# Attention scores moved out of PSUM by halves, a third bank for the other matmuls, and a wait on GpSimd

## The chip, the cores and the metric

The kernel runs on one core of a Trainium2 chip. The metric is the device time of one execution in microseconds (us), the median of several runs. A profiled execution, taken apart from these, gives the trace that the text reads. Engines are named as in the profile: PE is TensorE (matmuls), PEld its loading of weights, DVE VectorE, ACT ScalarE, POOL GpSimd, SP SyncE, which issues the DMAs.

## The reference

Two layers that have nothing to do with each other, written side by side. All data is fp32.

```python
def _A_ref(x, wqkv, wo):                       # x 1 x 2048 x 1024
    H = 32; Dh = D // H                        # 32 heads of 32
    q, k, v = ...(x @ wqkv)...                 # three projections
    scores = einsum("bhqd,bhkd->bhqk", q, k) * Dh ** -0.5
    p = softmax(scores, axis=-1)               # 2048 x 2048 for each head
    o = einsum("bhqk,bhkd->bhqd", p, v)
    return o.transpose(...).reshape(B, S, D) @ wo

def _B_ref(x, dft_seq_re, dft_seq_im, dft_hid_re, dft_hid_im):
    a = einsum("bsd,ed->bse", x, dft_hid_re)
    b = einsum("bsd,ed->bse", x, dft_hid_im)
    return einsum("ts,bse->bte", dft_seq_re, a) - einsum("ts,bse->bte", dft_seq_im, b)

return concatenate([_A_ref(...), _B_ref(...)], axis=-1)
```

## The kernel before

**Three kinds of work on TensorE.** Dense products (the projections of q, k and v, both products of the Fourier layer, the output projection) are done by a scheme of seven products for every block of 2 x 2. Each factor is split into a high and a low part of TensorE's fast fp32 format (`halves`: a cast `high`, line 477, and a subtraction `low`, line 480), and three matmuls stand for one. Sums of blocks that a product needs are made at line 455. These matmuls (line 391) are called *fills*; a group of 12 or 24 of them adds up in one PSUM bank of 128 x 512, and one VectorE instruction moves it out (lines 629 to 681, 894 to 907).

Attention goes by heads and has three streams. *S* (line 1198): a tile of scores, 128 queries by 1024 keys, in the PSUM tile `psS`. VectorE (line 1206) moves it to an SBUF row `srow`, negated, and takes the row minimum on the way into `negm`; ScalarE (line 1212) takes the exponentials, of which only the sums are used. So S gives each query's maximum and the sum of its exponentials. For head 0 VectorE only reduces (line 1208) and ScalarE works in PSUM (line 1214). *T* (line 1328): the transposed scores, keys by queries, with the maximum already taken off by two more rows of the product, in the banks `psT`; ScalarE makes the exponentials `pt`, `ptl` (line 1332). *V* (line 1347): products of these with V, 4096 short matmuls in all, 40, 40 and 48 in a block for each head; VectorE gathers the block into `ot` (lines 1358 and 1360).

S of head h + 1 runs while T and V of head h do, with fills between them. Before the first head there are only fills, and behind the last head the output projection.

**The order is planned while the program is written.** The class `Plan` simulates the engines with a duration for each operation (`MM`, `PV`, `SWITCH` and so on, in us) and emits each instruction when its engine is free in the plan and its inputs are ready. The chip then runs each engine's queue in that order, and semaphores hold an instruction until its inputs are there. The plan picks the next matmul from the heads of the streams S, T, V and the next fill, so that fills keep step with attention (the main loop, from line 1408). `LATE` and `SLATE` are how long the plan waits after the planned release of an input before it issues a matmul (`SLATE` for S). `OVERLAP` is what the next instruction of an engine may start early. A subtraction or a sum may go to GpSimd (`SUB`) or VectorE (`ADD`), whichever the plan finds free.

**The port.** Operations marked `two` use an SBUF port that VectorE and GpSimd share in the plan: `Plan.port` is the time at which it becomes free, and `choose` starts no GpSimd operation, nor a VectorE operation marked `two`, before that. On the chip nothing holds them apart in the kernel before: a GpSimd instruction starts when its own inputs are there.

**PSUM.** There are eight banks. Before: two tiles `psS` of two banks each, two banks `psT`, two banks `psD`. The tile `pd` of `psD` takes fills and V; `bank()` picks where a fill's group goes, and as long as attention isn't under way fills take `psT` too. The main loop keeps count of the banks in use (`banks`, at most 2, or 4 without attention).

Of the kernel before, what the change touches and what calls it, by code (L numbers as in the profile page):

```python
# [62 lines left out]
class Plan:  # L63
# [6 lines left out]
    OVERLAP = {"ACT": 0.13, "DVE": 0.08, "POOL": 0.08}  # L70
# [4 lines left out]
    QUEUE = 1.0  # L75

    def __init__(self):
        self.now = 0.0
        self.free = {e: 0.0 for e in ("PE", "ACT", "DVE", "POOL", "SP")}
        self.pending = {e: [] for e in ("ACT", "DVE", "POOL", "SP")}  # L80
        self.able = {e: [] for e in ("ACT", "DVE", "POOL", "SP")}
        self.dma = 0.0
        self.port = 0.0
        self.lane = [0.0] * 8
        self.seq = 0

# [39 lines left out]
    def start(self, o, e=None):  # L126
        e = e or o.engine
        o.emit(e) if o.other else o.emit()
# [83 lines left out]
def kernel(  # L212
# [79 lines left out]
    def load_qk(h, which, j):  # L292
# [12 lines left out]
        for n, b in (("psD", 2), ("psT", 2), ("psS", 2))  # L305
# [32 lines left out]
    MM, PV, SWITCH, TINY = 0.2275, 0.853, 0.40, 0.17  # L338
    ES, ET = 1.235, 0.625
    MOVE = 1.25  # L340
# [4 lines left out]
    LATE, SLATE = 0.25, 1.2  # L345
    HB = 0
    ACAST = 0.6
    RES = 400
    SST = 13
# [9 lines left out]
    pl = Plan()  # L359
    op = pl.op  # L360
# [56 lines left out]
    def fetch(shape, terms, store=None, keep=None):  # L417
# [23 lines left out]
        for sign, *term in terms[1:]:  # L441
# [12 lines left out]
            def add(e, sign=sign, other=other, a=None if last is not None else first[0]):  # L454
                (nc.gpsimd if e == "POOL" else nc.vector).tensor_tensor(  # L455
# [13 lines left out]
    def halves(raw, made, users, hi, lo, old, mine, order=(None, None)):  # L469
# [3 lines left out]
        def high(e=None):  # L473
            if e == "ACT":
                nc.scalar.activation(hi(), raw(), AF.Copy)
            else:
                nc.vector.tensor_copy(hi(), raw())  # L477

        def low(e):
            (nc.gpsimd if e == "POOL" else nc.vector).tensor_tensor(out=lo(), in0=raw(), in1=f(hi()), op=ALU.subtract)  # L480
# [679 lines left out]
    psS_r, psT_r, pt_r, vt_r, rt_r, ot_r = Ring(2), Ring(2), Ring(NPT), Ring(2), Ring(1), Ring(2)  # L1160
    small = {n: Ring(b) for n, b in (("st", 2), ("nm", 2), ("lh", 2), ("tw", 1))}
    qx_r = Ring(1)
    row_r = Ring(NROW)
    got = {}
# [7 lines left out]
    def scores(h):  # L1172
# [12 lines left out]
        for n, (qt, c) in enumerate([(k % 4, k // 4) for k in range(8)] + [divmod(k, 2) for k in range(8, 32)]):  # L1185
            old, users = psS_r.take()
            own = h > 0 and qt < 4
            box = {}
            if h:
                rold, ruse = row_r.take()  # L1190

            def mm(n=n, qt=qt, c=c, box=box, own=own):
                if n == 0:
                    ST["negm"] = sm.tile([P, 2, NS], F32, name="negm", bufs=2)
                    ST["sums"] = sm.tile([P, 2, NS], F32, name="sums", bufs=2)
                box["p"] = p = psS.tile([P, 1024], F32, name="psS")
                for i in range(2):
                    nc.tensor.matmul(  # L1198
                        p[:, i * NB : i * NB + NB], (QX[0] if own else QS[h % 2])[:, qt * P : qt * P + P],
                        KS[h % 2][:, c * 1024 + i * NB : c * 1024 + i * NB + NB], start=True, stop=True,  # L1200
                    )

            def mx(qt=qt, c=c, box=box):
                if h:
                    box["s"] = att_low().tile([P, 1024], F32, name="srow", bufs=NROW)
                    nc.vector.tensor_scalar(box["s"], box["p"], -1.0, None, op0=ALU.mult, op1=ALU.min, accum_out=ST["negm"][:, c, qt : qt + 1])  # L1206
                    return
                nc.vector.tensor_reduce(out=ST["negm"][:, c, qt : qt + 1], in_=box["p"], axis=AX.X, op=ALU.max, negate=True)  # L1208

            def ex(qt=qt, c=c, box=box):  # L1210
                if h:
                    nc.scalar.activation(box["s"], box["s"], AF.Exp, scale=-1.0, bias=ST["negm"][:, c, qt : qt + 1], accum_out=ST["sums"][:, c, qt : qt + 1])  # L1212
                    return
                nc.scalar.activation(box["p"], box["p"], AF.Exp, bias=ST["negm"][:, c, qt : qt + 1], accum_out=ST["sums"][:, c, qt : qt + 1])

            a = op("PE", 2 * MM, mm, [*old, *([got.get((h, "x"))] if own else [got.get((h, 0, qt // 4)), got.get((h, "z"))]), got.get((h, 1, 2 * c)), got.get((h, 1, 2 * c + 1))],
                   [users, xuse] if own else [users])
            b = op("DVE", MOVE if h else MAX, mx, [a] + (sold if n == 0 else []) + (rold if h else []), [users, suse, *([ruse] if h else [])], 0)
            e = op("ACT", ES, ex, [b], [ruse if h else users, suse], 0)
            exp_of[a] = e  # L1220
            maxes.append(b)
            exps.append(e)
            Sops.setdefault(h, []).append(a)
            streams["S"].append((a, h, n))
# [11 lines left out]
        def high():  # L1236
            box["l"] = sm.tile([P, 2, NS], F32R, name="lh", bufs=2)
            nc.vector.tensor_reduce(out=box["l"][:, 0], in_=ST["negm"].rearrange("p c n -> p n c"), axis=AX.X, op=ALU.min)

        def low():  # L1240
            nc.vector.tensor_tensor(out=box["l"][:, 1], in0=ST["nm"], in1=f(box["l"])[:, 0], op=ALU.subtract)
# [4 lines left out]
        def across():  # L1246
            box["t"] = sm.tile([P, 2 * NS], F32, name="lt", bufs=2)
# [11 lines left out]
    def sums(h):  # L1259
# [4 lines left out]
        def sub():  # L1264
            box["t"] = sm.tile([P, 2, NS], F32, name="tt", bufs=1)
            for c in range(2):
                nc.vector.tensor_tensor(out=box["t"][:, c], in0=ST["nm"], in1=ST["negm"][:, c], op=ALU.subtract)
# [250 lines left out]
```

## Time and profile before

| | us |
|---|---|
| median of 3 runs | 2990.05 (2988.33 to 2990.17) |
| profiled execution | 2990.43 |
| its span, first to last instruction | 2988.7 |
| PE busy | 2957.1 (99%) |
| DVE busy | 2395.0 (80%) |
| ACT busy | 2301.3 (77%) |
| POOL busy | 930.1 (31%) |
| mean granted TensorE clock | 0.998 of full speed |

The difference between the profiled execution and its span lies around the program. Matmuls are pipelined and the spans of two overlap, so a busy PE is not PE at its peak: what a matmul costs is read from the distance between the starts of two. A wait is shown with the engine whose work came last before it ended. Rows of groups read: line, engine, operation, output<-input, shapes, count | busy us, mean ns of one | idle us before them and who ended it. Rows of the timeline read: start us, duration us, engine, line, operation, count, and in brackets the idle time before it.

### The profile page before, as it was taken

How to read it: one execution, taken by the hardware profiler on the slowest of the kernel's cores; microseconds unless marked ns; L12 is line 12 of the kernel's file. 1: busy time of each engine (PE TensorE's matmuls, PEld its weight loads, DVE VectorE, ACT ScalarE, POOL GpSimd, SP SyncE). 2: the span in 40 equal slices, each digit the busy share in tenths (PEclk: the TensorE clock that was granted, in tenths of full speed). 3: DMA queues.
4: the chain of work that ended last, by engine and by line, in shares of the span. 5: the costliest groups of instructions: out<-in, count | busy, mean ns of one | idle time of the engine just before them, and what ended most of it. 6: DMA issues, size and time to landing. Idle time of an engine off the chain costs nothing.

```text
span 2988.7 us, 45652 instructions
## 1 busy us (share of the span) xinstructions
PE 2957.1 (99%) x14912; PEld 2145.3 (72%) x14912; DVE 2395.0 (80%) x4180; ACT 2301.3 (77%) x4316; POOL 930.1 (31%) x688
## 2 busy tenths in 40 slices
PE   9999999999999999999999999999999999999999
PEld 7887776677677677767776676777777767677787
DVE  7779788688877877887678888888787888887796
ACT  4336887888788888888888888888988888786321
POOL 2315345122212332222112353323212245343142
PEclk9999999999999999999999999999999999999999
DMA  9976657666626644554435675545433586466762
GB/s 338 360 233 201 200 180 249 193 219 218 209 68 200 203 148 142 180 179 145 139 110 155 197 240 170 165 152 171 129 112 99 185 267 211 149 187 200 266 207 99
DMA packets 376582, 558.59 MB, mean 187 GB/s; under 512 B 111100, under 2 KB 111100, under 8 KB 376220
## 3 DMA queue, kind: packets, MB, share of 16 engines
q1 hardware_dynamic: 376344, 555.68, 58.1%
q8 instruction: 117, 1.92, 0.3%
q14 instruction: 121, 0.99, 0.1%
HBM read 402.42 MB, written 153.11 MB: 186 GB/s over the span
## 4 chain that ended last, share of the span: by engine, by line
PE 90%; DVE 3%; ACT 3%; DMA 1%; issue 1%; SPq 0%; POOL 0%; DVEq 0%; POOLq 0%
PE pd L391 40%; PE pd L1347 15%; PE psT L1328 15%; PE psS L1198 14%; PE psT L391 7%; ACT srow L1212 2%; ACT pt L1332 1%; DVE srow L1206 1%; DVE slot L477 1%; DMA c<-u_d 0%; ACT ptl L1332 0%; DMA raw<-in_wd 0%; DVE negm L1208 0%; DVE h L477 0%; DMA rt<-r_d 0%
## 5 line engine op out<-in xcount | busy, mean ns | idle before, releaser
L1206 DVE TENSOR_SCALAR_CACHE_REDUCE srow<-psS 128x1024 f32<-128x1024 f32 x992 | 1203.1, 1220 | 211.2 <-ACT srow L1212 135.8
L1212 ACT ACTIVATE srow<-srow,negm 128x1024 f32<-128x1024 f32 x992 | 1197.1, 1214 | 15.1 <-DVE srow L1206 14.8
L1332 ACT ACTIVATE pt<-psT 128x512 f32<-128x512 f32 x1618 | 924.3, 643 | 254.9 <-PE psT L1328 238.1
L391 PE MATMUL pd<-slot,h 128*128 128x512 f32 x3352 | 1111.4, 391 | 4.8 <-DVE ot L1358 1.8
L1328 PE MATMUL psT<-qs,ks 128*128 128x512 f32 x2048 | 752.5, 396 | 5.6 <-ACT pt L1332 3.5
L391 PEld LDWEIGHTS pd<-slot,h 128*128 128x128 f32 x3352 | 630.1, 188 | 144.7 <-issue 4.2
L391 PE MATMUL pd<-slot,l 128*128 128x512 f32 x1676 | 654.4, 390 | 1.0 <-POOL l L480 1.0
L1328 PEld LDWEIGHTS psT<-qs,ks 128*128 128x128 f32 x2048 | 381.5, 188 | 157.5 <-ACT srow L1212 28.5
L480 POOL TENSOR_TENSOR l<-raw,h 128x512 fp32r<-128x512 f32 x167 | 226.1, 1355 | 796.0 <-DVE h L477 576.9
L1198 PE MATMUL psS<-ks,qs 128*128 128x512 f32 x1552 | 471.1, 391 | 1.3 <-DVE srow L1206 1.2
L1347 PE MATMUL pd<-pt,vt 128*32 128x512 f32 x3236 | 396.6, 597 | 1.6 <-DVE slot L896 1.1
L455 POOL TENSOR_TENSOR raw<-raw,g 128x512 f32<-128x512 f32 x221 | 295.7, 1344 | 317.8 <-issue 58.3
L391 PEld LDWEIGHTS pd<-slot,l 128*128 128x128 f32 x1676 | 315.2, 188 | 68.2 <-POOL l L480 1.8
L1198 PEld LDWEIGHTS psS<-ks,qs 128*128 128x128 f32 x1552 | 290.9, 188 | 63.9 <-DVE srow L1206 3.2
L1332 ACT ACTIVATE ptl<-psT 128x512 f32<-128x512 f32 x430 | 249.0, 639 | 109.7 <-PE psT L1328 102.8
L480 POOL TENSOR_TENSOR slot<-raw,slot 128x512 fp32r<-128x512 f32 x151 | 213.6, 1422 | 355.8 <-DVE slot L477 225.6
L1212 ACT ACTIVATION_READ_ACCUMULATOR srow<-srow,negm 128x1 f32 x992 | 257.7, 260 | 0.0
L1347 PEld LDWEIGHTS pd<-pt,vt 128*32 128x32 f32 x3236 | 102.3, 110 | 191.3 <-issue 182.4
L391 PE MATMUL pd<-slot,slot 128*128 128x512 f32 x768 | 189.6, 391 | 0.2 <-DVE e L681 0.2
L1360 DVE TENSOR_TENSOR ot<-ot,pd 128x512 f32<-128x512 f32 x64 | 43.9, 685 | 161.3 <-PE pd L1347 161.3
L1347 PE MATMUL pd<-ptl,vt 128*32 128x512 f32 x860 | 165.9, 600 | 4.2 <-DVE e L681 3.5
L391 PEld LDWEIGHTS pd<-slot,slot 128*128 128x128 f32 x768 | 144.2, 188 | 31.5 <-DVE e L681 0.5
(126 smaller groups left out, 2451.7 us busy)
## 6 DMA issues: line engine op xcount, KB each, us to landing
raw<-in_ct SPq DMA_DIRECT2D x224, 256.0 KB
g<-in_ct SPq DMA_DIRECT2D x128, 256.0 KB
qk_d<-e SPq DMA_DIRECT2D x52, 512.0 KB
qs<-qk_d SPq DMA_DIRECT2D x128, 192.0 KB
ks<-qk_d SPq DMA_DIRECT2D x128, 192.0 KB
raw<-ab_d SPq DMA_DIRECT2D x96, 256.0 KB
c<-u_d SPq DMA_DIRECT2D x88, 256.0 KB
g<-ab_d SPq DMA_DIRECT2D x80, 256.0 KB
```

The source lines that it names most:

```text
L391: nc.tensor.matmul(box["ps"], a[1]((a[0].hi, a[0].lo)[u]()), b[1]((b[0].hi, b[0].lo)[v]()), start=k == 0, stop=k == n - 1)
L455: (nc.gpsimd if e == "POOL" else nc.vector).tensor_tensor(out=dest(), in0=dest() if a is None else a.get(), in1=other["q"] if "q" in other ...
L477: nc.vector.tensor_copy(hi(), raw())
L480: (nc.gpsimd if e == "POOL" else nc.vector).tensor_tensor(out=lo(), in0=raw(), in1=f(hi()), op=ALU.subtract)
L1198: nc.tensor.matmul(p[:, i * NB : i * NB + NB], (QX[0] if own else QS[h % 2])[:, qt * P : qt * P + P], KS[h % 2][:, c * 1024 + i * NB : c * ...
L1206: nc.vector.tensor_scalar(box["s"], box["p"], -1.0, None, op0=ALU.mult, op1=ALU.min, accum_out=ST["negm"][:, c, qt : qt + 1])
L1212: nc.scalar.activation(box["s"], box["s"], AF.Exp, scale=-1.0, bias=ST["negm"][:, c, qt : qt + 1], accum_out=ST["sums"][:, c, qt : qt + 1])
L1328: nc.tensor.matmul(box["p"], KS[h % 2][:, t * P : t * P + P], QS[h % 2][:, j * NB : j * NB + NB], start=True, stop=True)
L1332: nc.scalar.activation(box["t"], box["p"], AF.Exp)
L1347: nc.tensor.matmul(po["p"][j * DH : j * DH + DH, :], VT[h][:, k, :], box["t"], start=(k == t0), stop=(k == t), tile_position=(0, j * DH),)
L1360: nc.vector.tensor_tensor(out=po["o"], in0=po["o"], in1=po["p"], op=ALU.add)
```

## The change

- A tile of scores is made in two halves of 512 keys, each in a PSUM bank of its own, of which there are three (`psS` 3 x 1 bank in place of 2 x 2). VectorE moves each half. The second half starts its minimum from what the first half left in `negm`, so it reads that value. The exponentials are still taken over the whole row of 1024 for heads 1 to 31. For head 0 VectorE writes the negated scores back to PSUM, and ScalarE takes the exponentials by halves; their sums are added up later.
- `psD`, for fills and V, has three banks in place of two; the main loop's counts follow (3 and 5).
- When the plan starts a GpSimd operation, and the last port-using VectorE operation that it started ends in the plan later than 2.5 us ago (`NEAR`), the GpSimd instruction gets a wait for that VectorE instruction (`behind`). For that, functions that emit now return their instruction.
- Planned durations: `PV` 0.853 to 0.86, `SWITCH` 0.40 to 0.30, `ES` 1.235 to 1.31 and `OVERLAP` of ACT 0.13 to 0.15, `ET` 0.625 to 0.64, `MOVE` 1.25 for a tile to 0.70 for a half, `ACAST` 0.6 to 0.63. `SLATE` 1.2 to 0.25, `SST` 13 to 14.
- The small tiles `lh` and `lt` have one buffer in place of two.

```diff
-    OVERLAP = {"ACT": 0.13, "DVE": 0.08, "POOL": 0.08}
+    OVERLAP = {"ACT": 0.15, "DVE": 0.08, "POOL": 0.08}
+    NEAR = 2.5
...
+        if e == "DVE" and o.two:
+            self.held = made, self.free[e]
+        elif e == "POOL" and self.held is not None and self.held[1] > self.now - self.NEAR:
+            self.behind(made, self.held[0])
...
-        for n, b in (("psD", 2), ("psT", 2), ("psS", 2))
+        for n, b in (("psD", 3), ("psT", 2), ("psS", 3))
...
-    MM, PV, SWITCH, TINY = 0.2275, 0.853, 0.40, 0.17
-    ES, ET = 1.235, 0.625
-    MOVE = 1.25
+    MM, PV, SWITCH, TINY = 0.2272, 0.86, 0.30, 0.17
+    ES, ET = 1.31, 0.64
+    MOVE = 0.70
...
-    LATE, SLATE = 0.25, 1.2
+    LATE, SLATE = 0.25, 0.25
-    ACAST = 0.6
+    ACAST = 0.63
-    SST = 13
+    SST = 14
...
+    pl.behind = lambda a, b: tc.add_manual_dep(a.ins, b.ins.name, ...)
...
-        if (not att_on[0] or not t_on[0]) and nbank[0] % 4 < 2:
+        if (not att_on[0] or not t_on[0]) and nbank[0] % 5 < 2:
...
-    psS_r, ... = Ring(2), ...
+    psS_r, ... = Ring(3), ...
...
+            for i in range(2):
+                old, users = psS_r.take()
+                k0 = c * 1024 + i * NB
+                def mm(...):
+                    box["p"] = psS.tile([P, NB], F32, name="psS")
+                    nc.tensor.matmul(box["p"], (QX[0] if own else QS[h % 2])[:, qt * P : qt * P + P], KS[h % 2][:, k0 : k0 + NB], start=True, stop=True)
+                def mx(...):
+                    m = ST["negm"][:, c, qt : qt + 1]
+                    nc.vector.tensor_scalar(row["s"][:, i] if h else box["p"], box["p"], -1.0, m if i else None, op0=ALU.mult, op1=ALU.min, accum_out=m)
+                a = op("PE", MM, mm, ...)
+                b = op("DVE", MOVE, mx, [a, *last] + ..., 0)
+            if h:
+                exp_of[a] = op("ACT", ES, ex, [b], [ruse, suse], 0)
+            for i, (a, box, users) in enumerate(() if h else halves_of):
+                exp_of[a] = op("ACT", ET + 0.15, ex0, [b], [users, suse], 0)
...
-        if len(banks) >= (2 if heads and t_on[0] else 4):
+        if len(banks) >= (3 if heads and t_on[0] else 5):
```

More of the change, by code (lines that the diff above doesn't have):

```diff
@@ L85, in __init__ @@
         self.seq = 0
+        self.held = self.behind = None
     def op(self, engine, cost, emit, after=(), uses=(), rank=0.0, kb=0, order=None, other=None, lanes=1, two=False):
@@ L127, in start @@
         e = e or o.engine
-        o.emit(e) if o.other else o.emit()
+        made = o.emit(e) if o.other else o.emit()
         o.begun = True
@@ L359 @@
     pl = Plan()
+    pl.behind = lambda a, b: tc.add_manual_dep(a.ins, b.ins.name, mybir.DependencyInfo(mybir.DependencyClass.Sync, mybir.DependencyReason.DATA), reason="port")
     op = pl.op
@@ L1185, in scores @@
         for n, (qt, c) in enumerate([(k % 4, k // 4) for k in range(8)] + [divmod(k, 2) for k in range(8, 32)]):
-            old, users = psS_r.take()
             own = h > 0 and qt < 4
-            box = {}
-            if h:
[L1190 to L1221, printed above, removed]
@@ L1266, in sub @@
             for c in range(2):
-                nc.vector.tensor_tensor(out=box["t"][:, c], in0=ST["nm"], in1=ST["negm"][:, c], op=ALU.subtract)
+                last = nc.vector.tensor_tensor(out=box["t"][:, c], in0=ST["nm"], in1=ST["negm"][:, c], op=ALU.subtract)
+            return last
         def ex():
```

60 lines of the change are left out of this document (43 added, 17 removed).

## The prediction

> **What bounds the kernel now.** I read the page first, then the chain that ended last, the windows of 100 us, the waits of TensorE, and last single lines and the timeline at the places where TensorE stood still.
>
> The page gives the busy times and the counts of the products with V:
>
> ```profile
> PE 2957.1 (99%) x14912; PEld 2145.3 (72%) x14912; DVE 2395.0 (80%) x4180; ACT 2301.3 (77%) x4316; POOL 930.1 (31%) x688
> ...
> L1347 PE MATMUL pd<-pt,vt 128*32 128x512 f32 x3236 | 396.6, 597 | 1.6 <-DVE slot L896 1.1
> ...
> L1347 PE MATMUL pd<-ptl,vt 128*32 128x512 f32 x860 | 165.9, 600 | 4.2 <-DVE e L681 3.5
> ```
>
> TensorE is busy throughout, but its spans overlap, so I build a floor from pitches. The chain shows undisturbed runs (start, length, what):
>
> ```profile
> 6.84 5.49 PE psT L391 x12
> ...
> 17.78 5.44 PE psT L391 x24
> ...
> 365.24 4.50 PE pd L1347 x40
> 388.34 4.43 PE pd L1347 x40
> 416.80 5.29 PE pd L1347 x48
> ```
>
> 24 plain matmuls take 5.44 us, 226.7 ns each. The three V blocks of a head take 4.50 + 4.43 + 5.29 = 14.22 us. There are 3236 + 860 = 4096 V matmuls (128 for each of 32 heads), so 14912 - 4096 = 10816 plain ones. Floor: 10816 x 0.2267 = 2452, plus 32 x 14.22 = 455, plus 6.8 before the first matmul, plus about 4 behind the last (below: 88.7 - 84.6): 2918 us. The span was 2988.7. So **71 us is all that any reordering can recover**. The change touches none of the 14912 matmuls; it can only move these 71, and 2.8 of them stay in any case: the first twelve matmuls take 5.49 where twelve others take 2.72.
>
> The windows (columns: PE, PEld, DVE, ACT, POOL busy with counts, granted clock, DMA share, GB/s) show where they lie:
>
> ```profile
> 200.00:300.00 100.00, 96.59 (x434) 75.08 (x433) 91.35 (x141) 65.59 (x117) 45.11 (x34) 0.98 0.62 198
> ...
> 400.00:500.00 100.00, 97.98 (x480) 69.91 (x479) 90.97 (x163) 84.67 (x161) 60.88 (x45) 0.98 0.73 238
> 500.00:600.00 100.00, 96.17 (x489) 63.89 (x488) 67.74 (x123) 76.25 (x145) 22.16 (x17) 0.97 0.69 213
> ...
> 2100.00:2200.00 100.00, 100.00 (x525) 71.38 (x524) 74.00 (x139) 88.02 (x167) 19.82 (x16) 1.00 0.39 120
> ...
> 2600.00:2700.00 100.00, 98.35 (x515) 69.52 (x514) 86.89 (x151) 78.57 (x148) 48.00 (x36) 1.00 0.58 176
> ...
> 2900.00:3000.00 100.00, 84.64 (x374) 69.78 (x372) 62.85 (x81) 14.02 (x24) 27.61 (x19) 0.99 0.29 103
> ```
>
> Where VectorE is at 74% and GpSimd at 20% (from 2100) TensorE loses nothing visible. Losses sit mostly where VectorE passes 85% (eight of the attention windows, from the one at 200 to the one at 2600) and GpSimd is at 45 to 61%. The window at 500 is another case, dealt with below. TensorE's waits:
>
> ```profile
> PE psT L1328 <- ACT pt L1332: 3.5, 10, 0.6
> PE pd L1347 <- DVE e L681: 3.5, 2, 2.8
> PE psS L1198 <- DVE srow L1206: 2.9, 3, 1.7
> ...
> PE pd L391 <- DVE ot L1358: 1.8, 1, 1.8
> PE pd L391 <- DVE ot L1360: 1.4, 1, 1.4
> ...
> PE pd L391 <- POOL l L480: 1.0, 2, 0.6
> ...
> PE pd L391 <- DVE e L681: 0.2, 1, 0.2
> ```
>
> Twelve rows name VectorE, from 3.5 down to 0.2; they sum to 15.4 us. GpSimd is named for 1.0. The rest of the 71 is in steps too short for this view.
>
> **GpSimd's wait for the port.** One such place, on three engines (start, duration):
>
> ```profile
> 779.79 0.42 DVE L477 CAST e<-e 128x512 fp32r<-128x512 f32 x1
> 780.12 3.28 DVE L477 CAST slot<-raw 128x512 fp32r<-128x512 f32 x3
> ...
> 780.01 1.35 POOL L480 TENSOR_TENSOR slot<-raw,slot 128x512 fp32r<-128x512 f32 x1 [0.83 <-DVE slot L477]
> ...
> 786.90 0.72 PE L1198 MATMUL psS<-ks,qs 128*128 128x512 f32 x2 [1.00 <-DVE srow L1206]
> ```
>
> GpSimd's subtraction starts at 780.01, as soon as its cast has landed. VectorE's next three casts, which take 0.42 alone, take 3.28 together; the queue behind them is late, and 6 us on TensorE stands for a score bank. The plan forbids this overlap, but nothing in the program did. Over the whole run:
>
> ```profile
> L477 DVE CAST h<-raw 128x512 fp32r<-128x512 f32 x321 | 157.7, 493 | 9.5 <-PE pd L391 6.6 <-PE psT L391 1.6 <-issue 1.2
> ...
> L477 DVE CAST slot<-raw 128x512 fp32r<-128x512 f32 x229 | 127.0, 571 | 3.4 <-DMA raw<-in_wd 2.1 <-POOL raw L455 0.3 <-PE pd L391 0.2
> ```
>
> ```profile
> L477 DVE CAST slot<-raw x229: 382/421/1549, 190.9 to 2921.3; 128x512 fp32r<-128x512 f32 x115
> ```
>
> Against the median of 421 ns the means say 229 x 0.150 + 321 x 0.072 = 57 us of VectorE lost in these casts alone. The new wait holds a GpSimd instruction behind the last port-using VectorE instruction that the plan put before it, if that ends less than 2.5 us earlier or later in the plan. It can't help where GpSimd itself is late (its data came late) and meets a later cast. I take half of it back: -28 us of VectorE (bounds -57 and 0). For TensorE: the wait at 786.90 is one of the three in the row srow L1206. I take that row and the two of ot to be of this kind, 2.9 + 1.8 + 1.4 = 6.1 us, and book **-5** (bounds -8, with the shorter rows, and 0). What queues behind the waiting GpSimd instruction are its other subtractions; who waits for them is TensorE's fills, and that cover is wide: 1.0 us of waits at 31% busy.
>
> The Trainium skill ("SBUF — State Buffer", Who interferes with whom) says that this port is locked for the whole instruction, that the one who came second is blocked fully, and that a tensor_scalar which also writes its accumulator takes no part. The casts' maximum of 1549 beside 421 agrees, and so does the move of scores below, whose longest is 5 ns over its median.
>
> **Moving scores 512 at a time.** Now one instruction of 1024 per tile (shortest, median and longest in ns, first and last start):
>
> ```profile
> L1206 DVE TENSOR_SCALAR_CACHE_REDUCE srow<-psS x992: 1181/1223/1228, 253.3 to 2713.2; 128x1024 f32<-128x1024 f32 x199
> ```
>
> ```profile
> 758.35 1.21 DVE L1206 TENSOR_SCALAR_CACHE_REDUCE srow<-psS 128x1024 f32<-128x1024 f32 x1
> ...
> 759.50 1.21 DVE L1206 TENSOR_SCALAR_CACHE_REDUCE srow<-psS 128x1024 f32<-128x1024 f32 x1
> ```
>
> ```profile
> 2612.26 0.67 DVE L1360 TENSOR_TENSOR ot<-ot,pd 128x512 f32<-128x512 f32 x1
> 2612.86 0.68 DVE L896 TENSOR_TENSOR slot<-slot,pd 128x512 f32<-128x512 f32 x1
> 2613.46 0.41 DVE L477 CAST h<-raw 128x512 fp32r<-128x512 f32 x1
> 2613.91 0.69 DVE L480 TENSOR_TENSOR l<-raw,h 128x512 fp32r<-128x512 f32 x1
> ```
>
> A tile takes 1.15 (759.50 - 758.35). No half move is in this trace; the nearest rows are 512-wide instructions out of PSUM: 0.60 from one to the next. Two halves: 1.20, if something stands between them. The second half reads the minimum that the first leaves, so back to back it waits: as the subtraction at 2613.91 does, which starts 0.04 after the 0.41 cast ends. That puts the second half at about 0.68 + 0.04 + some for the accumulator, 0.75, and the pair at 1.37. So +0.05 to +0.22 per tile, 992 times: +50 to +218 us of VectorE. I take +0.12, +119 us, since the plan starts the second half no sooner than 0.80 after the first and fills the hole if it has something. Net of the port VectorE gains 91: 2486, 83%. At 40 tiles per 100 us (992 between 253 and 2713) the dense windows go up by 4.8 points, less 1 for the port, to 95% at the worst. The cost to TensorE is queueing there: I book **+4**, a quarter of today's 15.4 (bounds 0 and the rival below).
>
> The Trainium skill ("VectorE: DVE Perf Modes", The DRAIN you can't avoid, and the rules at its end) speaks against the split: the next operation starts only when the pipeline is empty, so one should keep the number of operations small. By that a half would cost its full 0.68 and the sum would be the rival's. The rows above show a successor starting 0.07 before its forerunner's end.
>
> **Banks.** Scores hold three banks of 512 where they held two of 1024; the fourth goes to fills and V. The wait that this removes is the longest of all:
>
> ```profile
> 503.88 0.69 DVE L681 TENSOR_TENSOR e<-c,pd 128x512 f32<-128x512 f32 x1 [1.47 <-DMA c<-u_d]
> ...
> 504.62 1.93 PE L1347 MATMUL pd<-ptl,vt 128*32 128x512 f32 x8 [2.80 <-DVE e L681]
> ```
>
> V's first matmul wants a bank, the fill in it waits for VectorE, VectorE for a DMA. With a third bank V goes on. I book **-5**: 3.5 of this row and the shorter ones of its kind (bounds -8 and 0). For scores, a bank comes free after 0.6 instead of 1.15, but 1.5 tiles are held, not 2; with a late VectorE they fill sooner. I count that within the +4.
>
> **Durations, slack.** ScalarE, from the timeline:
>
> ```profile
> 1707.71 1.23 ACT L1212 ACTIVATE srow<-srow,negm 128x1024 f32<-128x1024 f32 x1
> ...
> 1708.85 1.16 ACT L1332 ACTIVATE pt<-psT 128x512 f32<-128x512 f32 x2
> 1709.80 1.24 ACT L1212 ACTIVATE srow<-srow,negm 128x1024 f32<-128x1024 f32 x1
> ```
>
> A row of exponentials takes 1.14 there, two of T 0.95. The old plan says 1.235 - 0.13 = 1.105 and 0.495 each, the new one 1.16 and 0.49: on the safe side for the first time. A V block of 40 is planned at 0.40 + 5 x 0.853 = 4.67 before, 4.60 after, against 4.43. Nearer numbers should mean fewer orders that turn out wrong; of the some 48 us that no row above names (71 less 15.4, 3.5, 1.0 and 2.8) I book **-7** (bounds +8 and -25: a new order can also be unlucky, and scores now start 0.25 instead of 1.2 behind the planned release of a bank).
>
> **Edits at nothing.** Head 0 gets two exponentials and a write-back per tile; its scores are spread over the opening in which fills keep TensorE going. If that cover failed, T would start later by 32 x (2 x 0.79 - 1.235) = 11 us of ScalarE time by the plan's own costs, and fills would still be there. One buffer instead of two for lh and lt is reused once a head, some 77 us apart (2460 / 32). No DMA is added or moved by hand.
>
> **Sum:** -5 + 4 - 5 - 7 = -13. The profiled execution took 2990.43 (span 2988.7 and 1.7 around it), 0.4 above the median of the runs, 2990.05; so **2977**.
>
> **Rivals.** (a) VectorE becomes the bound in the dense windows. Place: pairs of halves that stand back to back because the queue has nothing else ready. Price: 0.22 x 40 = 8.8 points; the eight windows above 85% go to 94 to 100%, where each lost microsecond of VectorE reaches TensorE through banks and late casts. At 3.5 us a window, the largest loss that a window shows today (500: 3.83), 28, less the 10 of port and bank: +18, 3008. It decides from about 0.17 a tile on without relief at the port. For it: 91% already at 200 and 400. Against: GpSimd has 69% free, and the plan moves subtractions there.
>
> (b) Gains and costs cancel: 2988. For it: most of the 71 us has no name that the edits answer to. (c) The new waits do not do what they say, because late data and not early starts make the collisions; then the -5 is gone, VectorE's +119 without relief costs TensorE 8 and not 4, and with the durations' unlucky bound of +8 the sum is -5 (banks) + 8 + 8 = +11: 3001; it decides where the waits of GpSimd for DMAs, not for casts, precede the long casts. (d) Better: accurate durations take half of the 71: 2955.
>
> **How the numbers follow.** Forecast (2966 to 2984) 0.43; (d) 0.15; (b) 0.15; (a) 0.17; (c) 0.10. A measurement here tells 0.2%, 6 us, from no change: faster is below 2984, 0.58; same 0.15; slower 0.27. The range for 8 in 10 leaves out half of (d) and the top of (a): 2957 to 3005.
>
> **What would show it.** Casts with a mean near 430 and fewer above 1000 ns; two moves of about 0.69 per tile, the second 0.60 to 0.75 after the first; VectorE at 82 to 85%; no wait of pd L1347 on L681 of over 1 us; TensorE's idle rows on VectorE at about 8 us. Wrong if VectorE passes 87%, if psS waits grow beyond 10 us, or if GpSimd's results turn up among TensorE's long waits.

## The result, and the profile after

The changed kernel takes 2982.27 us (median of 13 runs) against 2990.05 (13 runs): a ratio of 0.9976, 95% interval 0.9968 to 0.9985, or 7 to 8 us less. The forecast was 2977, and faster. The sign holds, and of the 13 us that were forecast somewhat over half came; what the change is made of came out quite otherwise, with parts of +15 to -30 us that nearly cancel.

The profiled execution took 2980.81, its span 2979.0. Its page, first section (share of the span and instructions by engine):

```profile
PE 2952.4 (99%) x14912; PEld 2145.4 (72%) x14912; DVE 2408.4 (81%) x6122; ACT 2312.3 (78%) x4379; POOL 1061.1 (36%) x829
```

VectorE has only 13 us more than before, though its moves alone grew by 214 (below). GpSimd has 141 instructions more: the plan moved subtractions and sums there. TensorE's waits after (total us, times, longest), all rows:

```profile
PE psT L398 <- ACT slot L482: 8.0, 2, 7.3
PE psT L1345 <- ACT ptl L1349: 4.0, 6, 1.1
PE psT L1345 <- ACT pt L1349: 2.5, 7, 0.5
PE psS L1207 <- DVE srow L1213: 2.2, 6, 0.6
PE pd L398 <- DVE h L483: 1.6, 1, 1.6
PE psT L398 <- DVE slot L486: 1.5, 2, 1.2
PE psS L1207 <- ACT psS L1233: 1.2, 3, 0.6
PE pd L398 <- POOL l L486: 0.2, 1, 0.2
```

VectorE is named for 5.3 us in place of 15.4. No V matmul (`pd L1364`) waits any more. The windows of 100 us that answer to those shown of before:

```profile
200.00:300.00 100.00, 92.76 (x382) 70.96 (x381) 86.06 (x226) 59.89 (x142) 41.00 (x32) 0.98 0.60 189
400.00:500.00 100.00, 100.00 (x522) 70.94 (x521) 93.06 (x244) 85.55 (x162) 61.67 (x49) 1.00 0.82 267
500.00:600.00 100.00, 100.00 (x516) 70.38 (x518) 78.38 (x217) 85.16 (x162) 24.44 (x19) 1.00 0.64 204
2100.00:2200.00 100.00, 100.00 (x529) 70.85 (x528) 77.38 (x212) 82.75 (x158) 23.21 (x18) 1.00 0.43 125
2600.00:2700.00 100.00, 100.00 (x525) 71.27 (x524) 85.86 (x226) 86.88 (x166) 50.84 (x40) 1.00 0.59 182
```

Between 400 and 500 VectorE is at 93%, and yet TensorE has no visible gap there; at 500 the 3.83 us are gone. From 200 to 300 it is worse than before: 92.76 against 96.59.

**One measure for all runs.** To place losses I summed, from the starts of the matmuls in each trace, what the distance between two exceeds its undisturbed value by, where that is over 30 ns. The undisturbed value is 227 ns; 319 into a V block; 522 out of one; within a block 409 to the next group of four, 8 within a group. The span less this sum is 2931 to 2935 us in all fourteen traces, so the sum accounts for the difference between any two to within 4 us. In the table "start" is from 200 to 300 us (head 0's scores end, T begins), "end" from 2800 on (last T, output projection), "between" 300 to 2800; what is missing to the sum (2 to 5 us) lies before 200. The gain is the ratio to runs of the kernel before that were taken with it, less one, times 2990; 95% intervals of the ratio are in brackets. Two rows are repeats: e8 came out as the same program as the changed kernel, and e11 as the same as e4, instruction for instruction. What differs between such two rows (5 us in the sum of the first pair) is what one trace differs from another by.

| run | gain us | ratio | lost, sum | start | between | end |
|---|---|---|---|---|---|---|
| before | | | 55.2 | 6.3 | 46.3 | 0 |
| after | -7 | 0.9976 [0.9968, 0.9985] | 44.1 | 13.4 | 24.3 | 3.5 |
| e1 after, no port wait | +20 | 1.0066 [1.0053, 1.0079] | 78.7 | 18.6 | 47.5 | 7.4 |
| e2 before + port wait | -18 | 0.9941 [0.9928, 0.9953] | 40.5 | 4.4 | 33.5 | 0 |
| e3 after, two banks counted | +15 | 1.0049 [1.0036, 1.0063] | 71.9 | 15.5 | 36.1 | 17.4 |
| e4 after, old durations | +13 | 1.0044 [1.0032, 1.0057] | 70.4 | 15.1 | 24.3 | 26.4 |
| e5 before + wait + durations | -13 | 0.9955 [0.9942, 0.9967] | 45.0 | 4.6 | 37.7 | 0 |
| e6 before + wait + split moves | -3 | 0.9990 [0.9981, 0.9998] | 50.4 | 6.6 | 41.8 | 0 |
| e7 e2, order redrawn | -17 | 0.9944 [0.9931, 0.9956] | 40.5 | 4.3 | 33.8 | 0 |
| e8 after, RES 410: same program as after | -10 | 0.9967 [0.9955, 0.9980] | 49.5 | 14.8 | 27.1 | 3.5 |
| e9 after, head 0 free | -16 | 0.9948 [0.9935, 0.9960] | 37.5 | 7.9 | 27.1 | 0 |
| e10 e2, wait always | -17 | 0.9943 [0.9929, 0.9956] | 40.2 | 4.3 | 33.6 | 0 |
| e11 e4, RES 800: same program as e4 | +15 | 1.0050 [1.0038, 1.0063] | 71.2 | 15.4 | 24.4 | 26.4 |
| e12 after, SLATE 1.2 | +30 | 1.0101 [1.0084, 1.0118] | 85.4 | 17.0 | 26.6 | 37.5 |

### The profile page after: what moved, and what is told of

Its sections match the earlier page's. It is cut to its first block, busy times and chain, and to the rows that moved or that the text cites. A ratio compares the mean times of both kernels' runs of the same rounds, so it can differ in the third digit from the quotient of the medians.

```text
span 2979.0 us, 49418 instructions
## 1 busy us (share of the span) xinstructions
PE 2952.4 (99%) x14912; PEld 2145.4 (72%) x14912; DVE 2408.4 (81%) x6122; ACT 2312.3 (78%) x4379; POOL 1061.1 (36%) x829
## 4 chain that ended last, share of the span: by engine, by line
PE 96%; DMA 1%; DVE 1%; ACT 1%; issue 0%; POOL 0%; SPq 0%; DVEq 0%; ACTq 0%; POOLq 0%
PE pd L398 44%; PE psT L1345 16%; PE psS L1207 15%; PE pd L1364 15%; PE psT L398 5%; DVE srow L1213 0%; ACT srow L1226 0%; ACT pt L1349 0%; DMA g<-in_wo 0%; DMA g<-in_ct 0%; DMA er<-in_xa 0%; DMA s<-o_d 0%; DMA t<-in_wo 0%; DMA t_d<-raw 0%; DMA vt<-v_d 0%
## 5 line engine op out<-in xcount | busy, mean ns | idle before, releaser
L398 PE MATMUL pd<-slot,h 128*128 128x512 f32 x3408 | 1181.4, 390 | 1.6 <-DVE h L483 1.6
L1345 PE MATMUL psT<-qs,ks 128*128 128x512 f32 x2048 | 797.1, 395 | 6.9 <-ACT ptl L1349 4.0
L1213 DVE TENSOR_SCALAR_CACHE_REDUCE srow<-psS,negm 128x512 f32<-128x512 f32 x992 | 738.9, 748 | 67.7 <-PE psS L1207 5.1
L1213 DVE TENSOR_SCALAR_CACHE_REDUCE srow<-psS 128x512 f32<-128x512 f32 x992 | 678.4, 687 | 94.5 <-ACT srow L1226 76.1
L1207 PE MATMUL psS<-ks,qs 128*128 128x512 f32 x1552 | 579.8, 392 | 3.3 <-DVE srow L1213 1.5
L486 POOL TENSOR_TENSOR l<-raw,h 128x512 fp32r<-128x512 f32 x223 | 288.7, 1296 | 707.0 <-DVE h L483 375.0
L462 POOL TENSOR_TENSOR raw<-raw,g 128x512 f32<-128x512 f32 x259 | 335.2, 1299 | 260.0 <-DVE raw L462 47.3
L1364 PE MATMUL pd<-pt,vt 128*32 128x512 f32 x3236 | 394.5, 594 | 0.0
L1364 PEld LDWEIGHTS pd<-pt,vt 128*32 128x32 f32 x3236 | 102.0, 110 | 187.3 <-issue 184.0
L1226 ACT ACTIVATION_READ_ACCUMULATOR srow<-srow,negm 128x1 f32 x992 | 232.3, 234 | 0.0
L398 PE MATMUL pd<-slot,slot 128*128 128x512 f32 x888 | 222.6, 391 | 0.0
L1207 PE MATMUL psS<-ks,qx 128*128 128x512 f32 x496 | 186.4, 397 | 0.8 <-DVE srow L1213 0.7
```

What stands on the lines that cost most here:

```text
L398: nc.tensor.matmul(box["ps"], a[1]((a[0].hi, a[0].lo)[u]()), b[1]((b[0].hi, b[0].lo)[v]()), start=k == 0, stop=k == n - 1)
L462: return (nc.gpsimd if e == "POOL" else nc.vector).tensor_tensor(out=dest(), in0=dest() if a is None else a.get(), in1=other["q"] if "q" i ...
L486: return (nc.gpsimd if e == "POOL" else nc.vector).tensor_tensor(out=lo(), in0=raw(), in1=f(hi()), op=ALU.subtract)
L1207: nc.tensor.matmul(box["p"], (QX[0] if own else QS[h % 2])[:, qt * P : qt * P + P], KS[h % 2][:, k0 : k0 + NB], start=True, stop=True)
L1213: nc.vector.tensor_scalar(row["s"][:, i] if h else box["p"], box["p"], -1.0, m if i else None, op0=ALU.mult, op1=ALU.min, accum_out=m)
L1226: nc.scalar.activation(r, r, AF.Exp, scale=-1.0, bias=ST["negm"][:, c, qt : qt + 1], accum_out=ST["sums"][:, c, qt : qt + 1])
```

## The experiments

### e1 and e2: the wait for the port, taken out of the one and put into the other

e1:

```diff
-    NEAR = 2.5
+    NEAR = -1e9
```

> The changed kernel without GpSimd's wait for the port, all else as changed; the plan and so the order in every queue are the same. Port theory (the wait gives VectorE back half of its blocked time and takes TensorE's long waits behind casts away): casts go back to means of 493 and 571 ns, some waits of 1 to 2 us on VectorE come back, 2987 to 2990 us. Rival (bank and durations made the gain, the wait only moves the blocked time to GpSimd): 2980 to 2984 us.

e2 adds to the kernel before:

```diff
+        if e == "DVE" and o.two:
+            self.held = made, self.free[e]
+        elif e == "POOL" and self.held is not None and self.held[1] > self.now - self.NEAR:
+            self.behind(made, self.held[0])
```

> The kernel before with GpSimd's wait for the port added and nothing else; again the same order in every queue. Port theory: the waits at 452, 760, 787 and 2613 us go (5.9 us of idle TensorE in all), and casts fall to means near 430 and 470 ns: 2982 to 2985 us. Rival (late data, not early starts, make the collisions): 2989 to 2991 us and the long casts stay.

e1 took 3012.11, e2 2975.22. Both miss the bounds that I had set, on the far side: the wait is worth 27 to 30 us in the changed kernel and 15 to 18 in the one before, three to six times what I booked. In neither pair does the order of any engine's instructions differ between the two traces, so nothing but the wait can be the cause. One sign missed: in e1 the casts rose to means of 476 (`h`) and 535 (`slot`), not to the 493 and 571 of before. First sections of e1 and e2:

```profile
PE 2972.2 (99%) x14912; PEld 2146.3 (71%) x14912; DVE 2463.2 (82%) x6122; ACT 2317.0 (77%) x4379; POOL 1094.5 (36%) x829
```

```profile
PE 2949.7 (99%) x14912; PEld 2148.2 (72%) x14912; DVE 2334.7 (79%) x4180; ACT 2297.8 (77%) x4316; POOL 880.4 (30%) x688
```

The wait does not move the blocked time to GpSimd: from before to e2 VectorE falls from 2395.0 to 2334.7 and GpSimd from 930.1 to 880.4. The casts into `slot`, in e2 and then in the changed kernel (means in ns behind the comma), against 571 before:

```profile
L483 DVE CAST slot<-raw 128x512 fp32r<-128x512 f32 x229 | 104.9, 474 | 4.6 <-DMA raw<-in_wd 1.9 <-PE psT L398 1.3 <-POOL raw L462 0.3
```

```profile
L483 DVE CAST slot<-raw 128x512 fp32r<-128x512 f32 x227 | 103.8, 467 | 4.6 <-DMA raw<-ab_d 1.8 <-PE pd L398 1.8 <-PE psT L398 0.7
```

The place that the prediction showed, in e2's timeline, VectorE and GpSimd:

```profile
770.85 0.42 DVE L483 CAST e<-e 128x512 fp32r<-128x512 f32 x1
771.18 1.09 DVE L483 CAST slot<-raw 128x512 fp32r<-128x512 f32 x3
```

```profile
773.00 3.82 POOL L486 TENSOR_TENSOR slot<-raw,slot 128x512 fp32r<-128x512 f32 x3 [2.78 <-PE pd L1354]
```

The three casts take 1.09 where they took 3.28; GpSimd does its subtractions behind them. Casts are only half of it: from before to e2 the two groups of casts named in the prediction fall by 32 us (284.7 to 252.6), VectorE in all by 60. Most of the rest is in its sums and subtractions, which the wait shortened too; those of `slot<-raw,slot`, for one, go from 805 to 750 ns in the mean.

TensorE's waits on VectorE in e2, the three longest rows (three more have 0.5 or less):

```profile
PE pd L398 <- DVE e L687: 3.5, 1, 3.5
PE pd L398 <- DVE h L483: 3.5, 3, 2.1
...
PE psT L1335 <- DVE e L635: 1.1, 1, 1.1
```

Together the six rows have 9.2 us, where the kernel before has 15.4.

Without the wait the changed kernel shows where late VectorE work lands, in e1's waits:

```profile
PE psS L1207 <- DVE srow L1213: 12.5, 22, 1.7
```

against 2.2 in 6 with it. The kernel before, which has no wait for the port either, loses 2.9 us in 3 there. So scores stand less of a late VectorE in the changed kernel, and the wait is worth more. Whether that comes of the smaller banks, of the slack of 0.25 in place of 1.2, or of VectorE's fuller queue (2463 us busy against 2395) is not shown.

### e7 and e8: RES 410, to draw the order anew

```diff
-    RES = 400
+    RES = 410
```

> The kernel before with the wait for the port, and one number without a meaning of its own for this question changed, RES from 400 to 410, which shifts the points at which fills are preferred. It shows how much the time moves when only the order is drawn anew: 2971 to 2980 if orders hardly matter, outside of that if the luck of an order is as large as the effects that are compared.

> The changed kernel with RES 410 in place of 400. Again only the order is drawn anew: 2978 to 2987 if orders hardly matter; above 2990 or below 2974 if the luck of an order is as large as the effect of the whole change.

2973.26 and 2981.80: within 2 us of 2975.22 and 2982.27. Only e7 is a new order, and a mild one: at 738 of the 14912 places in TensorE's queue stands another matmul than in e2. e8 is the changed kernel itself, since RES decides nothing in it, so it tells how well a measurement repeats and nothing about orders. How much luck of the order there is in the changed kernel, and in e3, e4, e6 and e12, which all have orders of their own, was not measured.

### e3: the third bank

```diff
-        if len(banks) >= (3 if heads and t_on[0] else 5):
+        if len(banks) >= (2 if heads and t_on[0] else 5):
```

> The changed kernel, but the main loop lets only two of the three banks be in use by fills and V during attention (the count 3 goes back to 2). Bank theory: V's first matmul waits for a bank again, 8 to 10 us in all as before: 2989 to 2993 us. Rival (any order with the wait for the port does as well): 2980 to 2985 us.

3006.07, past both ranges: the count of three is worth 22 to 24 us, more than I expected even of the bank theory. Nor does that theory's sign come back: no V matmul (`pd L1364`) is in e3's list of TensorE's waits, and by the measure above the delays in front of V's matmuls grow only from 0.3 to 3.6 us in all. The plan itself holds V and new groups of fills back while it counts no free bank, so the price turns up elsewhere. The table parts it into 12 between (9 against the repeat, e8) and 14 at the end. There a single wait takes most:

```profile
PE pd L398 <- ACT slot L482: 9.9, 1, 9.9
```

It is the output projection's first group behind the last V block. The last T starts at 2823.5 us in this run (2796.3 in the changed kernel, 2785.8 before), and no fill is left to cover what lies between the last head's result and the projection's first input.

### e6: the split by itself

The kernel with the port wait, scores in its two tiles of two banks, but moved by two instructions:

```diff
-    MOVE = 1.25
+    MOVE = 1.58
...
-                    nc.vector.tensor_scalar(box["s"], box["p"], -1.0, None, op0=ALU.mult, op1=ALU.min, accum_out=...)
+                    m = ST["negm"][:, c, qt : qt + 1]
+                    for i in range(2):
+                        u = slice(i * NB, i * NB + NB)
+                        nc.vector.tensor_scalar(box["s"][:, u], box["p"][:, u], -1.0, m if i else None, op0=ALU.mult, op1=ALU.min, accum_out=m)
```

> The kernel before with the wait for the port, and VectorE moves each tile in two dependent instructions of 512 out of the same two-bank tile; the plan counts 1.50 for the pair. It takes the price of the split by itself, without its banks. The trace of the changed kernel has 0.82 from the first half to a second one right behind it and 0.68 from there on, 1.50 against 1.15, so VectorE gets about 350 us more less what moves to GpSimd. Theory that VectorE becomes the bound in dense windows: TensorE loses 10 to 25 us more, 2985 to 3000. Rival (GpSimd takes subtractions over and TensorE sees nothing): 2973 to 2979 with GpSimd well over its 688 instructions.

2985.60, at the lower edge of the theory's range: the split costs some 10 to 15 us here (lost time 50.4 against 40.5). Timeline of VectorE in e6, one pair of halves (start, duration):

```profile
1458.04 0.68 DVE L1215 TENSOR_SCALAR_CACHE_REDUCE srow<-psS 128x512 f32<-128x512 f32 x1
1458.64 0.09 DVE L1215 DVE_READ_ACCUMULATOR srow<-psS 128x1 f32 x1
1458.77 0.75 DVE L1215 TENSOR_SCALAR_CACHE_REDUCE srow<-psS,negm 128x512 f32<-128x512 f32 x1
1459.44 0.08 DVE L1215 DVE_READ_ACCUMULATOR srow<-psS,negm 128x1 f32 x1
```

0.73 from the first half to the second and 0.67 from there on, 1.40 where one move took 1.15; and the half that reads a scalar is 0.07 longer than the other. Its first section:

```profile
PE 2948.4 (99%) x14912; PEld 2143.1 (72%) x14912; DVE 2474.9 (83%) x6070; ACT 2303.6 (77%) x4315; POOL 1001.8 (34%) x783
```

VectorE gets 140 us more than in e2 although 95 instructions moved to GpSimd. GpSimd takes over, then, and TensorE sees the split nonetheless. But the waits do not say that VectorE became the bound: the rows that name it sum to 8.3 us here and to 9.2 in e2. What grows is T behind ScalarE, in e2 and then here:

```profile
PE psT L1335 <- ACT pt L1339: 2.4, 6, 0.6
```

```profile
PE psT L1338 <- ACT pt L1342: 8.8, 15, 0.9
```

That ScalarE is late because its rows of scores come late from VectorE, or because the plan with MOVE 1.58 drew another order, are both possible; neither was tried. From here to the changed kernel the loss between 300 and 2800 falls from 41.8 to 24.3 (27.1 in e8); by e3 the banks do part of that, the slack and the new durations perhaps the rest.

### e5, e4, e11, e12: the durations and the slack

e5 puts the new numbers into e2, e4 the old ones into the changed kernel (the diff is e4's, lines between left out):

```diff
-    OVERLAP = {"ACT": 0.15, "DVE": 0.08, "POOL": 0.08}
+    OVERLAP = {"ACT": 0.13, "DVE": 0.08, "POOL": 0.08}
...
-    MM, PV, SWITCH, TINY = 0.2272, 0.86, 0.30, 0.17
-    ES, ET = 1.31, 0.64
+    MM, PV, SWITCH, TINY = 0.2275, 0.853, 0.40, 0.17
+    ES, ET = 1.235, 0.625
...
-    LATE, SLATE = 0.25, 0.25
+    LATE, SLATE = 0.25, 1.2
...
-    ACAST = 0.63
+    ACAST = 0.6
...
-    SST = 14
+    SST = 13
```

> The kernel before with the wait for the port and the new durations (SLATE and SST among them; MOVE stays 1.25 for a tile of 1024, scores stay in two tiles of two banks). The wait alone gave 2975. Durations theory (nearer numbers give better orders): 2965 to 2972. Rival (they only draw another order, and 0.25 of slack hurts where a bank takes 1.15 to move): 2973 to 2990, with waits of psS on VectorE above 5 us.

> The changed kernel with the durations of before (ES, ET, PV, SWITCH, ACAST, OVERLAP of ScalarE, SLATE, SST; MOVE stays 0.70). Durations theory: the plan orders S and T too early for ScalarE, the 7 us booked for them go, and with a bank's slack of 1.2 instead of 0.25 scores come later: 2987 to 2992 us. Rival (durations only draw another order): within 4 us of the changed kernel, 2978 to 2986 us, with the stalls at other places.

e5: 2977.80, no gain over e2 (2975.22), with the waits that the rival named:

```profile
PE psS L1204 <- DVE srow L1212: 6.0, 8, 1.7
```

e4: 3005.05, 20 to 23 us worse than the changed kernel, and outside both expectations. Between 300 and 2800 it loses the same 24.3; the difference is the end. T in the changed kernel and in e4 (shortest, median, longest ns, first and last start), and e4's window at the end:

```profile
L1345 PE MATMUL psT<-qs,ks x2048: 387/389/792, 276.2 to 2796.3; 128*128 128x512 f32 x187
```

```profile
L1345 PE MATMUL psT<-qs,ks x2048: 387/389/796, 298.1 to 2822.6; 128*128 128x512 f32 x187
```

```profile
2800.00:2900.00 100.00, 86.01 (x370) 58.30 (x370) 52.71 (x79) 40.52 (x71) 22.74 (x18) 0.88 0.54 195
```

T starts at 298 in place of 276 and ends at 2823 in place of 2796; then TensorE has nothing but T, at ScalarE's pace. I first took it that too few fills were kept:

```diff
-    RES = 400
+    RES = 800
```

> The changed kernel with the old durations, as in the run of 3005 us, and RES 800 in place of 400, so that more fills are kept for the end of attention. In that run TensorE lost 26 us after 2800 us, in the last head's T and before the output projection, against 3.5 in the changed kernel, and the same 24 us between 300 and 2800. Theory (durations cost only through fills that ran out): loss after 2800 below 8 us, 2982 to 2990. Rival (the old durations misplace work throughout): above 2995 whatever is kept.

3005.38, with the same end and the same places: RES 800 gives the same program as 400 did. The reserve decides nothing there, so no more fills were kept, and this run is a repeat of e4 that says nothing of its theory. e12 asks which number does it:

```diff
-    LATE, SLATE = 0.25, 0.25
+    LATE, SLATE = 0.25, 1.2
```

> The changed kernel with SLATE alone put back from 0.25 to 1.2. All the old numbers together gave 3005, with 26 us lost after 2800 us. Theory (a slack of 1.2 behind the release of each of three single banks holds scores back, attention ends some 20 us later and fills run out before the output projection can start): 2998 to 3008, most of it lost after 2800 us. Rival (the durations of exponentials and of V did it): 2980 to 2986.

3019.93: the slack alone, and more than all old numbers together.

```profile
L1345 PE MATMUL psT<-qs,ks x2048: 387/389/796, 299.8 to 2836.8; 128*128 128x512 f32 x187
```

```profile
2800.00:2900.00 100.00, 84.47 (x340) 47.68 (x329) 39.61 (x60) 45.33 (x78) 16.81 (x13) 0.83 0.50 180
```

With three single banks a slack of 1.2 at each of 64 releases per head holds scores back, at head 0 most of all: T starts 24 us later than in the changed kernel and ends 40 us later. So of the two values of SLATE the single banks need 0.25. With 1.2 the old durations are even some 15 us better than the new ones (e4 against e12). The old durations with SLATE 0.25 were not run, so what the durations are worth without the slack stays open.

### e9: head 0

```diff
+                    if not h:
+                        m = ST["negm"][:, 2 * c + i, qt : qt + 1]
+                        nc.vector.tensor_reduce(out=m, in_=box["p"], axis=AX.X, op=ALU.max, negate=True)
+                        return
...
-                b = op("DVE", MOVE, mx, [a, *last] + ...
+                b = op("DVE", MOVE, mx, [a, *(last if h else [])] + ...
```

with four columns of maxima and sums for head 0 instead of two, and `lt`, `ll` and `nm` shared to make room.

> The changed kernel, but for head 0 each half of 512 keeps its own maximum and sum (four columns that the closing step combines, where the changed kernel has two running ones), so VectorE only reduces, nothing is written back to PSUM, and a bank goes to ScalarE without waiting for the other half. The changed kernel loses 13 us of TensorE's time between 200 and 300 us, the kernel before 6. Theory (head 0's scores hold the three single banks, so T starts 14 us later and finds no fills): this loss falls to about 5 and the time to 2973 to 2977. Rival (the loss there is ScalarE's on T, whatever head 0 does): 2979 to 2985, the loss stays above 10.

2974.77, 7.5 us better than the changed kernel.

```profile
200.00:300.00 100.00, 95.79 (x447) 69.98 (x446) 85.67 (x204) 79.55 (x176) 31.59 (x24) 1.00 0.49 151
```

```profile
L1346 PE MATMUL psT<-qs,ks x2048: 387/389/505, 245.9 to 2768.1; 128*128 128x512 f32 x187
```

T starts 30 us sooner and ends 28 us sooner; the start loses 7.9 in place of 13.4 and the end nothing in place of 3.5. The start stays above the 5 that I expected. This is a version that beats both kernels (0.9948), level with e2, e7 and e10 within the intervals; e10 ran on the same chip against the same runs of the kernel before.

### e10: what collisions are left

```diff
-    NEAR = 2.5
+    NEAR = 1e9
```

in e2.

> The kernel before with the wait for the port, and no limit of 2.5 us: every GpSimd instruction waits for the last port-using VectorE instruction planned before it, however long ago. The order is that of the kernel with the wait alone (2975.2), where 66 us of VectorE's time still go in instructions that are longer than their median. Theory (VectorE runs late against the plan by more than 2.5 us): blocked time below 45 us and 2969 to 2973. Rival (GpSimd is the late one, because its data is): blocked time 60 to 70 us and 2974 to 2977.

2973.19, just above the theory's range and just below the rival's, 2 us from e2, and the casts as in e2:

```profile
L483 DVE CAST slot<-raw 128x512 fp32r<-128x512 f32 x229 | 104.9, 474 | 3.8 <-PE psT L398 1.3 <-DMA raw<-in_wd 1.3 <-POOL raw L462 0.3
```

Waiting for VectorE longer back removes nothing more from the casts, which speaks for the rival. That GpSimd is the late one in what remains, and because of its data, fits but was not tried by itself.

## Why the prediction was right, and where not

**The floor and the bound.** 2918 plus what reordering can recover, 71, was the frame. In the fourteen traces the span without its losses is 2931 to 2935, and the losses are 37 to 85. The floor was some 15 too low: 9 of that is the way into the 96 V blocks (319 ns to the next start where 227 is usual), which the blocks' own lengths do not hold, and the rest is a few ns at each matmul. The bound was in truth about 55.

**The port, booked at -5.** Right in kind: the same casts at the same place, 1.09 for 3.28. Wrong in size: -15 to -18 by itself, -27 to -30 inside the changed kernel. The step that failed is the count. I summed TensorE's rows that name VectorE, and the rows did about what I booked: from before to e2 they fall from 15.4 to 9.2 us. But the time that TensorE lost fell by 14.7 (55.2 to 40.5), so more than half of the gain is in delays that the rows do not show: a matmul's span is 0.39 us or more where the next one starts after 0.227, so a delay shorter than the overlap leaves no idle time. On VectorE I priced the casts alone, where the wait gave about as much back on sums and subtractions. The cast means were forecast as near 430, which does not go with the -28 that I booked (half of 57 leaves them near 473); they came to 452 and 467, so casts fell by 37, two thirds of the 57. And of the eight windows in which VectorE passes 85%, GpSimd is at 45 to 61% in five only; in the other three it is at 31 to 36%.

**The split, booked at +4.** The halves on VectorE, from the timeline of the changed kernel, first with a cast between them, then back to back:

```profile
274.10 0.68 DVE L1213 TENSOR_SCALAR_CACHE_REDUCE srow<-psS 128x512 f32<-128x512 f32 x1
...
274.71 0.42 DVE L483 CAST e<-e 128x512 fp32r<-128x512 f32 x1
275.05 0.75 DVE L1213 TENSOR_SCALAR_CACHE_REDUCE srow<-psS,negm 128x512 f32<-128x512 f32 x1
...
275.71 0.69 DVE L1213 TENSOR_SCALAR_CACHE_REDUCE srow<-psS 128x512 f32<-128x512 f32 x1
...
276.53 0.75 DVE L1213 TENSOR_SCALAR_CACHE_REDUCE srow<-psS,negm 128x512 f32<-128x512 f32 x1
...
277.21 0.42 DVE L483 CAST h<-raw 128x512 fp32r<-128x512 f32 x1
```

With a cast between, the halves take 0.61 and 0.66; back to back 0.82 and 0.68, 1.50 against my upper bound of 1.37. Reading the minimum as a scalar makes the second half 748 ns in the mean where the first has 687; that I had not priced. In all, moves are busy 1417 us (738.9 + 678.4) in place of 1203.1. VectorE did not reach the 82 to 85% that I forecast (81%), because 141 sums and subtractions left it and the wait for the port gave some 60 us back (e2). On TensorE e6 prices the split at 10 to 15 us. Rival (a) had the pairs of halves back to back, but not the path to TensorE: in the window from 400 VectorE is at 93% and TensorE shows no gap, and in e6 the rows of T behind ScalarE grow, not those of VectorE. The rule of the Trainium skill ("VectorE: DVE Perf Modes", Rules for kernel authors) to keep the number of operations small, which I cited against the split, points the right way. The reason that I took from its section on the DRAIN, that an operation starts only when the pipeline is empty, does not hold here: 0.61 from a half of 0.68 to the cast behind it. That section itself adds that an operation which is not held starts earlier.

**The banks, booked at -5.** V's waits are gone from the rows, as forecast, but the step from the wait at 504.62 to a missing bank is not borne out. In e2, with two banks, V waits 0.4 us at that place, and 27 us later a fill waits 3.5 for the same kind of move, on the chain that ended last:

```profile
515.73 5.48 DMA c<-u_d
521.33 0.70 DVE e L687
522.07 0.80 PE pd L398
```

Behind the move stands the DMA into `c`, as it did at 503.88 in the kernel before; VectorE stood idle 4.6 us for it. In the changed kernel VectorE waits 0.6 us in all for this DMA, and in e3, with two banks counted, 2.4; in neither does TensorE wait for the move. So another order takes this wait away as well as a bank. What the third bank is worth is 22 to 24 (e3), by a path that I did not forecast: attention ends 27 us sooner, and fills last to the end.

**Durations and slack, booked at -7.** Durations and slack together gave nothing that shows in the kernel with the wait (e5), and they were not tried apart there. The slack, which I put among the risks ("scores now start 0.25 instead of 1.2 behind"), is what makes single banks work: 1.2 costs 37 us with them (e12).

**Head 0, booked at nothing.** Wrong: 7.5 us (e9). I named fills as the cover, and they covered TensorE in part (13.4 us lost from 200 to 300, for 6.3 before). T starts 14 us later than before (276 for 262), near the 11 that I gave for the case that the cover fails. What I left out is that fills used there are missing later, and that T cannot start before head 0's maxima are known. A delay at the start moves the whole of attention, and the end pays too.

**The sum.** -13 against -7 measured. Port -15 to -18, split +10 to +15, banks -9 to -24, head 0 about +8, each taken in another kernel, so that they do not add up to one sum. The total was near because errors on both sides cancelled, and that was luck. The price that decided the forecast's sign, the port, had the right sign by the right evidence. The wait alone (e2, 2975) does better than the whole change: with it in place, all other edits together cost 7 to 10 us.

## What to carry to other kernels

Where an engine is busy 99%, measure distances between its starts, not its idle time: of the 55.2 us that TensorE lost here in the kernel before, the rows of its waits behind the first matmul name 19.9. Where a planner forbids two engines to overlap on a shared resource, the program has to enforce it: here a wait on the engine with slack (GpSimd, 31% busy) cost nothing that shows, while an instruction blocked on the loaded one delayed all behind it. A change to buffers must be followed through the first and the last pass of a loop as well: from e6 to the changed kernel the steady part lost 15 to 18 us less, and head 0 and the last head gave 10 to 12 of it back.

## What the runs showed of the hardware

After a long wait TensorE is slow for some microseconds. In the kernel before, the V block behind the 2.80 us wait at 504.62, on the chain that ended last, and the same block in e2, where that wait is 0.4:

```profile
504.62 8.38 PE pd L1347 x48
```

```profile
495.25 5.36 PE pd L1354 x48
```

The block takes 3.0 us more than in e2, on top of the wait. The granted clock from 504 to 513 us in the kernel before (the number behind the five engines' busy times, 0.64):

```profile
504.00:513.00 9.00, 8.38 (x49) 2.02 (x50) 3.34 (x6) 0.00 (x0) 1.28 (x1) 0.64 0.95 278
```

The first twelve matmuls of the program, 5.49 for 2.72, are as slow, but the profile has no lower clock there, so that the clock is the reason at that place is not shown. The Trainium skill ("TensorE: Matmul & The Clock Gate", Part 1) says that the array falls to half its clock after an idle window of about 3.4 us; here it was down after a wait of 2.8. So this wait cost about twice its length. In the changed kernel the clock falls once within the work (0.98 from 200 to 300 us), and no wait of TensorE there is longer than 1.1 us; several of these stand close together.

This is part of the losses in the table. The mean granted clock of the profiled runs is 0.999 for the changed kernel, 0.995 for e1 and e3, 0.993 for e4 and 0.991 for e12, which is 0.4 to 0.8% of some 3000 us. So by an estimate up to 12 us in e1 and e3, 18 in e4 and 24 in e12 of what they lose beyond the changed kernel is the lower clock that follows waits, and not the waits themselves. It is a bound: a slow matmul that would have waited anyway costs nothing.
